# Second layer of a two-layer FFN as one scheme of 26 block products, its weight sums kept in device memory and streamed

## The chip, the cores and the metric

One core of a Trainium2 chip runs the whole program. The metric is device microseconds of one execution. The kernel before takes 1073.24 us, the median of 7 runs (1072.73 to 1074.44). Five engines run side by side: PE (TensorE, matmuls), DVE (VectorE), ACT (ScalarE), POOL (GpSimd) and SP (SyncE, which only issues DMAs here). Each executes its own instructions in the order of the program, and waits on semaphores for the others. DMAs are issued from a queue of SP, POOL or ACT, in order, and land later.

## The reference

```
kv  = einsum('bhsd,bhse->bhde', k, v)          # 8 batches, 8 heads, 576 tokens, 64 dims
o   = einsum('bhsd,bhde->bhse', q, kv)
x   = o / sqrt(mean(o*o, -1) + 1e-6) * g_norm  # then (B,H,S,D) -> (4608, 512)
h   = sigmoid(x @ w_gate) * (x @ w_val)        # 512 -> 1536
out = h @ w_out                                # 1536 -> 512
```

Everything is float32 on the chip; the three weights arrive as 64-bit floats and are converted.

## The kernel before

The 4608 tokens are nine chunks `c` of G = 512. Attention makes x, transposed, chunk by chunk (`feed`); chunk 0 is computed plainly, with the weights converted beside it. From chunk 1 on both layers use sums of blocks, so that fewer products are needed, as in Strassen's scheme and its kin: one 2x2 scheme of seven products, with a further level on one of them.

The first layer (`first_layer_fast`, loop `f` = 0..5, a "pass" each) makes two blocks of h at a time, `f` and `f + 6`, each [128 features, 512 tokens], in 24 matmuls of 256 columns and 7 of 128. Its sums of w_gate and w_val are made once, on POOL, in chunk 1 (`w_sum`, `w_sums2`, lines 729 to 746), stored in device memory (`kept`, `kept2`) and loaded again for every pass of later chunks (`load_sums`, L724 to L727, DMAs of 1 MB and 256 KB on POOL's queue). One addition of each pass is on POOL (L836); it waits for ACT's copies (L835), and DVE's L844 waits for it, and PE for that. The blocks end with products by the sigmoid on DVE (`end`, L800) and additions out of PSUM (L796). Then `h_sum` and `h_sums` (L880 to L889) make the sums of h for the second layer, four DVE operations of 128x256 a pass.

The second layer (`second_layer_fast`) has 60 matmuls of 256 columns and 42 of 128 a chunk (L920, L979); the small ones need sums that POOL makes during this stage (`sums2`, L909, 48 operations of 128x128). The sums of w_out (`t2w`, L1099 to L1106) are made once, on DVE, during chunk 1's first layer, and stay on the core. The last chunk has its own form, `second_layer_last`, with 72 matmuls of 256 columns and 24 of 128, ordered so that little is left to store at the end.

Beside this, the attention of a later batch is fed in steps: `fill` is a list of small steps, and `slot()` emits the next of them at marked places of both layers. A step on PE is the kv group (L355, L361) or one of two groups of 144 small matmuls (L396). `load_late` loads k and v of batch c + 2 at the end of a second layer, on SP's queue behind the stores of the results (`store`, L500). Tiles `gv`, `s12`, `s4` and `kv` come from one rotating pool of 21 buffers (`hp`), the tiles of the results and of the gates from `sg_tile` (5 buffers). PSUM banks are handed around by `take` and `give`: a bank is reused when DVE or ACT has read it.

What sets the order is thus the program's order on each engine, with these steps spread in it by hand; there is no scheduler (`manual_schedule`).

## Time and profile before

| | us |
|---|---|
| median of 7 runs | 1073.24 |
| the profiled execution | 1074.33 |
| its span, first to last instruction | 1072.5 |
| PE busy | 1059.7 |
| DVE busy | 671.6 |
| POOL busy | 311.8 |
| ACT busy | 307.4 |
| moved by DMA | 127.94 MB, mean 119 GB/s |

Line numbers (L753) are those of the kernel before. Names stand as out<-in. A float32 matmul shows as two MATMUL records, and each record's end is modelled, so that the distance of starts, not the length of a record, is its price. "Idle before" is the time for which an engine had nothing to run, with what ended it. SPq and POOLq are the issuing queues. The granted clock of PE is 1.00 in all windows.

### The profile page before, as it was taken

The numbers are of one execution on the slowest core, as the hardware profiler recorded it, in microseconds if no ns is written. First come the engines' busy times: TensorE is split into PE (matmuls) and PEld (weight loads), VectorE is DVE, ScalarE is ACT, GpSimd is POOL, SyncE is SP. The second block draws the span as 40 slices with busy tenths as digits, with TensorE's granted clock in tenths as the row PEclk, the third lists the DMA queues.
The fourth block names the chain that finished last, engine by engine and source line by source line (L and its number), as shares of the span: only waits on it lengthen the run. The fifth ranks groups of instructions, "written<-read, shape, count | busy, mean of one in ns | idle before, by whom it ended". The sixth has DMA issues, their size and how long they took to land.

```text
span 1072.5 us, 20227 instructions
## 1 busy us (share of the span) xinstructions
PE 1059.7 (99%) x7766; PEld 890.5 (83%) x7766; DVE 671.6 (63%) x1545; ACT 307.4 (29%) x737; POOL 311.8 (29%) x576
## 2 busy tenths in 40 slices
PE   8999999999999999999999999999999999999998
PEld 7644448788988898889988898889888988898887
DVE  4787766996556646675568466755566466626641
ACT  3654322331133303331243123311333032102210
POOL 0000045888111531145112711181115211631100
PEclk9999999999999999999999999999999999999999
DMA  9944712234433426341634263334333232312201
GB/s 247 265 158 156 237 62 96 99 123 139 138 114 121 133 63 198 111 133 41 182 110 135 80 186 101 121 96 122 126 123 120 55 106 99 99 40 99 99 1 39
DMA packets 85056, 127.94 MB, mean 119 GB/s; under 512 B 26976, under 2 KB 66272, under 8 KB 82272
## 3 DMA queue, kind: packets, MB, share of 16 engines
q1 hardware_dynamic: 70112, 63.66, 21.3%
q0 software_dynamic: 14496, 62.92, 17.1%
q8 instruction: 61, 1.00, 0.4%
q14 instruction: 35, 0.29, 0.1%
q10 hardware_dynamic: 352, 0.07, 0.0%
HBM read 102.24 MB, written 17.30 MB: 111 GB/s over the span
## 4 chain that ended last, share of the span: by engine, by line
PE 95%; DVE 2%; POOL 1%; DMA 1%; SPq 1%; issue 0%; POOLq 0%; DVEq 0%
PE mm L753 45%; PE mm L920 17%; PE mm L558 7%; PE mm L757 7%; PE mm L979 6%; PE mm L655 4%; PE mm L1030 3%; PE at L396 2%; PE at L355 1%; DMA v<-in_v_dram 1%; PE at L558 1%; PE two L262 0%; POOL tws L744 0%; PE two L292 0%; PE two L319 0%
## 5 line engine op out<-in xcount | busy, mean ns | idle before, releaser
L753 PE MATMUL mm<-xT,w 128*128 128x256 f32 x720 | 177.2, 379 | 0.0
L753 PE MATMUL mm<-sx,w 128*128 128x256 f32 x720 | 177.1, 379 | 0.0
L753 PEld LDWEIGHTS mm<-xT,w 128*128 128x128 f32 x720 | 133.0, 190 | 16.5 <-issue 0.5
L753 PEld LDWEIGHTS mm<-sx,w 128*128 128x128 f32 x720 | 132.0, 190 | 15.3
L836 POOL TENSOR_TENSOR sg<-sg 128x256 f32<-128x256 f32 x48 | 34.8, 724 | 322.6 <-ACT sg L835 303.1
L753 PE MATMUL mm<-xT,tws 128*128 128x256 f32 x432 | 113.1, 384 | 1.1 <-DVE gv L776 0.6
L753 PE MATMUL mm<-sx,tws 128*128 128x256 f32 x432 | 111.3, 380 | 0.1
L766 ACT COPY sg<-mm 128x256 f32<-128x256 f32 x96 | 36.0, 375 | 241.9 <-PE mm L753 241.5
L772 DVE TENSOR_TENSOR gv<-mm,sg 128x256 f32<-128x256 f32 x96 | 40.3, 423 | 91.6 <-PE mm L753 85.2
L753 PEld LDWEIGHTS mm<-xT,tws 128*128 128x128 f32 x432 | 77.1, 190 | 13.0 <-issue 3.0
L791 ACT ACTIVATE sg<-sg 128x256 f32<-128x256 f32 x96 | 40.0, 416 | 158.1 <-DVE sg L790 157.8
L753 PEld LDWEIGHTS mm<-sx,tws 128*128 128x128 f32 x432 | 75.7, 191 | 8.0 <-PE mm L753 1.2
L800 DVE TENSOR_TENSOR gv<-gv,sg 128x256 f32<-128x256 f32 x192 | 80.2, 438 | 0.0
L558 PE MATMUL mm<-xT,w 128*128 128x512 f32 x176 | 77.4, 594 | 0.0
L920 PE MATMUL mm<-w,s 128*128 128x256 f32 x336 | 73.7, 379 | 0.0
L920 PEld LDWEIGHTS mm<-w,s 128*128 128x128 f32 x336 | 63.8, 190 | 8.7
L776 DVE TENSOR_TENSOR gv<-mm,sg 128x256 f32<-128x256 f32 x96 | 40.5, 422 | 45.0 <-PE mm L753 39.1
L558 PEld LDWEIGHTS mm<-xT,w 128*128 128x128 f32 x176 | 32.6, 190 | 37.4 <-issue 35.9
L744 POOL TENSOR_TENSOR tws<-w 128x256 f32<-128x256 f32 x24 | 19.4, 827 | 151.9 <-DVE w L202 146.9
L790 DVE TENSOR_TENSOR sg<-mm,sg 128x256 f32<-128x256 f32 x96 | 40.3, 420 | 33.2 <-PE mm L753 32.8
L776 DVE TENSOR_TENSOR gv<-mm,gv 128x256 f32<-128x256 f32 x96 | 40.6, 423 | 27.7 <-PE mm L753 26.4
L757 PEld LDWEIGHTS mm<-xT,w 128*128 128x128 f32 x276 | 43.0, 191 | 6.6 <-DVE gv L796 3.3
(158 smaller groups left out, 1835.5 us busy)
## 6 DMA issues: line engine op xcount, KB each, us to landing
w<-kept POOLq DMA_DIRECT2D x21, 1024.0 KB, 6.1
tws<-kept POOLq DMA_DIRECT2D x21, 1024.0 KB, 5.2
out_dram<-sg SPq DMA_DIRECT2D x110, 64.0 KB, 1.7
q<-in_q_dram SPq DMA_DIRECT2D x24, 288.0 KB, 3.1
st<-in_moe_w_gate_dram SPq DMA_DIRECT2D x12, 512.0 KB, 3.7
st<-in_moe_w_val_dram SPq DMA_DIRECT2D x12, 512.0 KB, 7.7
st<-in_moe_w_out_dram SPq DMA_DIRECT2D x12, 512.0 KB, 4.4
kv<-in_k_dram SPq DMA_DIRECT2D x24, 256.0 KB, 5.0
```

Of the source, the lines that this page charges most:

```text
L558: nc.tensor.matmul(self.ps[i], w[("wg", "wv")[i], self.f][:, m, :], xT[self.c][:, m, :], start=(m == 0), stop=(m == NMT - 1), skip_group_c ...
L655: nc.tensor.matmul(ps[t], gv[0, f][:, P * t:P * t + P], w["wo", f], start=(f == 0), stop=(f == NFT - 1), skip_group_check=True)
L753: nc.tensor.matmul(ps, wt[:, m, :], xs[:, m, :], start=(new and m == 0), stop=(m == NK - 1), skip_group_check=True)
L757: nc.tensor.matmul(ps, wt, xs, start=new, stop=True, skip_group_check=True)
L766: nc.scalar.copy(out=d["sg"][:, h2], in_=d["pa"])
L772: tt(out=d["h"][:, h1], in0=d["pb"], in1=d["sg"][:, h2], op=ALU.add)
L776: tt(out=d["h"][:, h2], in0=ps, in1=d.pop("u")[:, h2], op=ALU.add)
L790: tt(out=d["sg"][:, h2], in0=d["pb"], in1=d["sg"][:, h2], op=ALU.add)
L791: nc.scalar.activation(out=d["sg"][:, h2], in_=d["sg"][:, h2], func=AF.Sigmoid)
L800: tt(out=d["h"][:, h], in0=d["h"][:, h], in1=d["sg"][:, h], op=ALU.mult)
L920: nc.tensor.matmul(ps, hs[f], ws[:, f, :], start=(new and f == 0), stop=(f == NF2 - 1), skip_group_check=True)
L979: nc.tensor.matmul(ps, hs[j], ws[j], start=(new and j == 0), stop=(j == N3 - 1), skip_group_check=True)
```

## The change

From chunk 2 on the second layer is one scheme with h as 4x4 blocks (four token tiles of 128 by four groups of three feature blocks, numbers 4t + l) and w_out as 4x2 blocks: 26 products (`PRODUCTS`), each three matmuls of 256 columns. Each product reads a block or a sum of blocks of h (`H_SUMS`, 28 sums for each of three feature blocks `j`, 128x128, all on POOL) and a block or a sum of blocks of w_out (`W_SUMS`, 18 sums). The h sums are emitted two at a time at the places of the first layer (`step`), for j = 0 and 1, and three at a time between the first ten products for j = 2. The w_out sums are made on DVE during chunk 1's second layer and stored in device memory (`kept3`); each chunk streams them back in the order of the products, 384 KB each, into a ring of seven places (`ring`, `load_w`), on POOL's queue. Chunk 1's second layer becomes plain, 48 matmuls of 512 columns; `second_layer_last`, `sums2`, `h_sum`, `h_sums` of before, `t2w` and their steps are gone. The h blocks get fixed places (`h_main`, `h_more`), k and v use `h_more` too (`kv_place`), and `sg_tile` has 6 buffers.

```diff
-                mains[n, name] = t = hp.tile([P, G], FP32, tag="gv", name="kv")
+                mains[n, name] = t = kv_place(len(mains))
...
-        rest = hp.tile([P, G], FP32, tag="gv", name="kv")
+        rest = kv_place(len(mains))
...
+    N3 = NF2 // 2
+    def block(l, j):
+        return 2 * j + l % 2 + NF2 * (l // 2)
     def gv_tile(c, f):
-        gv[c, f] = hp.tile([P, G], FP32, tag="gv", name="gv")
+        e, r = divmod(f, NF2)
+        l, j = 2 * e + r % 2, r // 2
+        gv[c, f] = h_main[j][:, NT * l:NT * l + NT].rearrange("p t c -> p (t c)")
         return gv[c, f]
+    def kv_place(i):
+        return h_more.rearrange("p j s c -> p (j s c)")[:, G * i:G * i + G]
     def sg_tile():
-        return sb.tile([P, G], FP32, tag="sg", name="sg", bufs=5)
+        return sb.tile([P, G], FP32, tag="sg", name="sg", bufs=6)
...
-                hp = ctx.enter_context(tc.tile_pool(name="hp", bufs=21))
+                hp = ctx.enter_context(tc.tile_pool(name="hp", bufs=1))
+                h_main = [hp.tile([P, 4 * NT, P], FP32, name=f"h{j}") for j in range(N3)]
+                h_more = hp.tile([P, N3, 3 * NT, P], FP32, name="h_more")
...
+        def step():
+            slot()
+            for _ in range(2):
+                if h_fill:
+                    h_fill.popleft()()
...
             if load:
                 load_sums(c + (n == 0), n)
-            slot()
+            if c == 2 and f:
+                for n_ in range(f, NR + 1, NF2 - 1):
+                    load_w(n_ - 1)
+            step()
...
             p6(two)
-            slot()
+            step()
...
-            h_sum(c, f)
             p3(two)
-            slot()
+            step()
             end(one, h1)
             end(two, h1)
-            h_sums(c, f)
+            if c > 1 and f % 2:
+                h_fill.extend(h_sums(f // 2))
         if c + 1 < NG:
             load_sums(c + 1, 1)
...
+    H_SUMS = ((18, 5, 1, 6), (21, 0, -1, 2), (24, 8, 1, 21), (17, 9, -1, 13), (26, 14, -1, 17), (25, 1, 1, 18),
+              (16, 11, -1, 15), (23, 12, -1, 16), (30, 26, -1, 10), (33, 21, 1, 23), (19, 3, 1, 11), (27, 1, 1, 19),
+              (42, 12, 1, 15), (34, 13, 1, 27), (35, 14, 1, 34), (36, 1, 1, 3), (20, 4, -1, 6), (22, 12, 1, 20),
+              (29, 8, 1, 25), (41, 0, 1, 29), (37, 4, 1, 12), (28, 7, 1, 18), (40, 28, -1, 16), (38, 7, 1, 20),
+              (39, 19, 1, 38), (32, 1, 1, 5), (31, 17, -1, 22), (43, 10, -1, 24))
+    W_SUMS = ((9, 1, 0, 1, 4), (12, 1, 3, -1, 9), (22, 1, 7, 1, 12), (14, -1, 2, -1, 9), (23, 1, 6, -1, 14),
+              (8, 1, 5, -1, 6), (21, 1, 4, -1, 8), (16, 1, 1, 1, 8), (18, 1, 2, -1, 16), (15, 1, 3, -1, 0),
+              (20, 1, 8, -1, 15), (10, 1, 5, -1, 7), (13, -1, 1, -1, 10), (25, 1, 3, 1, 13), (11, 1, 0, 1, 2),
+              (17, 1, 1, -1, 11), (19, -1, 10, -1, 11), (24, 1, 1, 1, 5))
+    PRODUCTS = (("A", 8, 4, "o5=A"), ("C", 9, 1, "o4=C"), ("B", 18, 10, "o3=B"), ("A", 24, 14, "o1=A"),
+                ("C", 26, 16, "t8=C"), ("B", 25, 19, "o1=o1+B"), ("E", 23, 12, "t9=E"), ("C", 30, 6, "o5=o5-C"),
+                ("A", 33, 9, "t9=t9+A"), ("F", 27, 13, "t0=F"), ("E", 16, 22, ""), ("B", 19, 25, "t0=B-t0"),
+                ("H", 42, 3, "t9=t9-H o4=o4-t9 o0=t9+t0"), ("F", 35, 24, ""), ("G", 36, 7, "t1=G t1=F-t1"),
+                ("D", 20, 15, "o2=D"), ("G", 2, 23, "o1=G-o1 o2=o2+t0 o5=o5+t1 o7=t1-E"), ("D", 22, 20, "o3=o3+D"),
+                ("I", 41, 11, "o0=o0+I o1=o1-I"), ("E", 37, 21, ""), ("E", 40, 7, "o3=o3+E"), ("J", 39, 3, ""),
+                ("J", 32, 17, "o2=J-o2"), ("D", 31, 8, "t8=t8+D o7=o7-t8"), ("K", 43, 2, "o4=o4+K"),
+                ("H", 14, 18, "o6=H+t8"))
+    DONE = {18: 0, 22: 1, 24: 2, 25: 3}
+    LAST = {"A": 8, "B": 11, "C": 7, "D": 23, "E": 20, "F": 14, "G": 16, "H": 25, "I": 18, "J": 22, "K": 24}
+    def h_slots():
+        used, last = {p[1] for p in PRODUCTS}, {}
+        for n, (_, x, _, y) in enumerate(H_SUMS):
+            last[x] = last[y] = n
+        at = {4 * t + l: NT * l + t for t in range(NT) for l in range(4)}
+        spare = deque(at[v] for v in range(16) if v not in last and v not in used)
+        top = 16
+        for n, (v, x, _, y) in enumerate(H_SUMS):
+            spare.extendleft(at[u] for u in (y, x) if last[u] == n and u not in used)
+            if spare:
+                at[v] = spare.popleft()
+            else:
+                at[v], top = top, top + 1
+        assert top <= 16 + 3 * NT
+        return at
+    h_at = h_slots()
+    h_fill = deque()
+    def h_form(v, j):
+        s_ = h_at[v]
+        return h_main[j][:, s_] if s_ < 4 * NT else h_more[:, j, s_ - 4 * NT]
+    def h_sums(j):
+        return [lambda v=v, x=x, sign=sign, y=y: nc.gpsimd.tensor_tensor(
+            out=h_form(v, j), in0=h_form(x, j), in1=h_form(y, j), op=ALU.add if sign > 0 else ALU.subtract)
+            for v, x, sign, y in H_SUMS]
+    tok = [slice(P * i, P * i + P) for i in range(NT)]
+    def w_raw(v):
+        n, l = divmod(v, 4)
+        b0 = block(l, 0)
+        return w2[:, b0:b0 + NF2 - 1:2, DH * n:DH * n + DH]
+    STREAM = [p[2] for p in PRODUCTS if p[2] > 7]
+    NS = len(STREAM)
+    NR = 7
+    N_FAST = NG - 2
+    def ring(i):
+        i %= NR
+        return w_raw((0, 5)[i]) if i < 2 else w_ring[:, i - 2]
+    def load_w(i):
+        if i < N_FAST * NS:
+            nc.gpsimd.dma_start(out=ring(i), in_=kept3[i % NS].rearrange("p (j n) -> p j n", j=N3))
+    def w_forms():
+        last = {}
+        for n, (_, _, x, _, y) in enumerate(W_SUMS):
+            last[x] = last[y] = n
+        more = h_more.rearrange("p j s c -> p (j s c)").rearrange("p (i j n) -> p i j n", j=N3, n=DH)
+        spare = deque([w_ring[:, i] for i in range(NR - 2)] + [more[:, i] for i in range(2 * N3)])
+        at = {v: w_raw(v) for v in range(8)}
+        steps = []
+        for n, (v, sx_, x, sy, y) in enumerate(W_SUMS):
+            at[v] = spare.popleft()
+            for u in {x, y, v}:
+                if u > 7 and last.get(u, n) <= n:
+                    spare.append(at[u])
+            def make(v=v, sx_=sx_, x=x, sy=sy, y=y, o=at[v], a=at[x], b=at[y]):
+                op = ALU.add if sy > 0 else ALU.subtract
+                if sx_ > 0:
+                    tt(out=o, in0=a, in1=b, op=op)
+                else:
+                    nc.vector.scalar_tensor_tensor(out=o, in0=a, scalar=-1.0, in1=b, op0=ALU.mult, op1=op)
+                nc.gpsimd.dma_start(out=kept3[STREAM.index(v)].rearrange("p (j n) -> p j n", j=N3), in_=o)
+            steps += [make, idle]
+        return steps
+    def second_layer_plain(c):
+        for t in range(NT):
+            i = free.popleft()
+            ps = bank(i)
+            order_ = [block(l, j) for j in range(N3) for l in (0, 2, 1, 3)]
+            for f in order_:
+                nc.tensor.matmul(ps, gv[c, f][:, tok[t]], w2[:, f, :], start=(f == order_[0]), stop=(f == order_[-1]),
+                                 skip_group_check=True)
+                slot()
+            ot = sg_tile()
+            nc.scalar.copy(out=ot, in_=ps)
+            give(i)
+            store(c, t, ot)
+        flush()
+        load_late(c + 2)
     def second_layer_fast(c):
+        o = {}
+        tiles = [sg_tile() for _ in range(6)]
+        rows = [tiles[i] for i in (0, 1, 2, 4)]
+        for t in range(NT):
+            for n in range(2):
+                o[f"o{2 * t + n}"] = rows[t][:, DH * n:DH * n + DH]
+        for i, names in ((3, ("t8", "t9")), (5, ("t0", "t1"))):
+            for n, name in enumerate(names):
+                o[name] = tiles[i][:, DH * n:DH * n + DH]
+        regions, streamed = {}, count((c - 2) * NS)
+        state = {}
+        def product(i, js):
+            name, hv, wv, _ = PRODUCTS[i]
+            if i not in state:
+                if name not in regions:
+                    regions[name] = take() + (True,)
+                state[i] = next(streamed) if wv > 7 else None
+                new = regions[name][2]
+                regions[name] = regions[name][:2] + (False,)
+                state[i] = state[i], new
+            g, new = state[i]
+            ws = w_raw(wv) if g is None else ring(g)
+            for j in js:
+                nc.tensor.matmul(regions[name][1], h_form(hv, j), ws[:, j], start=(new and j == 0), stop=(j == N3 - 1),
                                  skip_group_check=True)
+        def finish(i):
+            name, _, wv, steps = PRODUCTS[i]
+            o.update({r: v[1] for r, v in regions.items()})
+            for step in steps.split():
+                out_, expr = step.split("=")
+                if expr in regions:
+                    nc.scalar.copy(out=o[out_], in_=o[expr])
+                else:
+                    sign = "+" if "+" in expr else "-"
+                    x, y = expr.split(sign)
+                    tt(out=o[out_], in0=o[x], in1=o[y], op=ALU.add if sign == "+" else ALU.subtract)
+            for r in list(regions):
+                if i == LAST[r]:
+                    give(regions.pop(r)[0])
+            g = state[i][0]
+            if g is not None:
+                load_w(g + NR)
+            if i in DONE:
+                t = DONE[i]
+                if c == NG - 1 and t == NT - 1:
+                    store(c, t, rows[t], slice(0, DH), (nc.sync, nc.scalar))
+                else:
+                    store(c, t, rows[t])
+            elif c == NG - 1 and i == 23:
+                store(c, NT - 1, rows[NT - 1], slice(DH, DM))
+        first = 3
+        for i in range(first):
+            product(i, range(N3 - 1))
+        for i in range(len(PRODUCTS)):
+            for _ in range(3):
+                if h_fill:
+                    h_fill.popleft()()
+            product(i, [N3 - 1] if i < first else range(N3))
+            finish(i)
...
+    kept3 = kept_pool.tile([NS, P, N3 * DH], FP32, name="kept3")
...
-    def t2w_sum(i, in0, in1):
-        for fs in (slice(f, f + 2) for f in range(0, NF2, 2)):
-            w2_sums.append(lambda fs=fs: tt(out=t2w[i][:, fs], in0=in0[:, fs], in1=in1[:, fs], op=ALU.subtract))
-
-    t2w_sum(3, b22, b12)
-    t2w_sum(1, b12, b11)
-    t2w_sum(2, b22, t2w[1])
-    t2w_sum(4, b21, t2w[2])
-
-
+    w_ring = sums.tile([P, NR - 2, N3, DH], FP32, name="w_ring", bufs=1)
...
         if c + 1 < B:
-            steps = feed(c + 1)
-            if c == 1:
-
-                i = 4
-                while w2_sums:
-                    steps.insert(i, (DVE, w2_sums.popleft()))
-                    i += 2
-            spread(steps, (1, 2, 3, 4, 5) if c == 1 else (2, 3, 4, 5))
+            spread(feed(c + 1), (1, 2, 3, 4, 5) if c == 1 else (2, 3, 4, 5))
         first_layer_fast(c)
         sums_of(c + 1)
-        (second_layer_fast if c < NG - 1 else second_layer_last)(c)
+        if c == 1:
+            fill.extend(w_forms())
+        (second_layer_plain if c == 1 else second_layer_fast)(c)
         flush()
```

## The prediction

> **What bounds the kernel.** I read the page's engine row and chain first, then the windows of the stages, then the chain in order of time for the price of one matmul record, and last the timelines of GpSimd (POOL) and SyncE.
>
> ```profile
> PE 1059.7 (99%) x7766; PEld 890.5 (83%) x7766; DVE 671.6 (63%) x1545; ACT 307.4 (29%) x737; POOL 311.8 (29%) x576
> ...
> PE 95%; DVE 2%; POOL 1%; DMA 1%; SPq 1%; issue 0%; POOLq 0%; DVEq 0%
> ```
>
> TensorE carries 95% of the chain, so the change is worth what it takes from PE's columns, less any new wait of PE. The windows are chunk 1's first and second layer, then the second layers of chunks 2, 7 and 8 (columns: length, then each engine's busy time):
>
> ```profile
> 161.59:245.14 83.55, 79.89 (x597) 67.10 (x596) 71.17 (x139) 27.54 (x77) 62.60 (x96) 1.00 0.32 114
> 245.14:283.35 38.21, 37.80 (x349) 33.94 (x348) 21.79 (x55) 4.14 (x8) 21.20 (x48) 1.00 0.31 91
> ...
> 360.27:397.77 37.50, 37.50 (x349) 33.99 (x348) 19.98 (x49) 4.06 (x7) 21.46 (x48) 1.00 0.32 87
> 924.83:960.27 35.44, 35.44 (x205) 32.34 (x204) 15.93 (x37) 1.35 (x4) 22.86 (x48) 1.00 0.15 47
> 1031.81:1068.41 36.60, 36.60 (x193) 32.69 (x191) 6.80 (x19) 1.49 (x4) 0.00 (x0) 1.00 0.10 24
> ```
>
> Second layers have no idle PE, and the granted clock is 1.00. The one stage with slack to win is chunk 1's first layer: 83.55 us, where chunk 2's takes 76.92 with the same matmuls plus one attention group (L396).
>
> ```profile
> 120.55 41.20 PE mm L655 x96
> ...
> 474.01 6.47 PE mm L920 x30
> 480.48 1.84 PE at L396 x130
> 482.32 19.62 PE mm L920 x90
> 501.94 9.63 PE mm L979 x84
> ```
>
> A float32 matmul is two records. One record costs 19.62 / 90 = 0.218 us (6.47 / 30 = 0.216) at 256 columns, 9.63 / 84 = 0.115 at 128, 41.20 / 96 = 0.429 at 512.
>
> **PE's columns.** Chunks 2 to 7: before, 120 records of 256 and 84 of 128, 25.9 + 9.6 = 35.5 (the window of chunk 7 says 35.44). After: 26 products of 3 matmuls, 156 records x 0.2157 = 33.65. That is -1.80 a chunk, **-10.8** for six (between -1.6 by the 0.218 and -1.9). Chunk 8: 36.60 becomes 33.65, **-2.95**. Chunk 1 becomes plain: 48 matmuls of 512 columns, 96 x 0.429 = 41.2, where the window of 38.21 less its attention group (37.50 - 35.44 = 2.06, by chunks 2 and 7) was 36.15: **+5.05**. The attention group is not lost: in the built order of PE both groups of chunk 1 now lie in its first layer, at the same cost.
>
> **Chunk 1's first layer.** Its PE work is six passes of 11.96 us (24 matmuls of 256, 7 of 128), 2.4 for kv and 1.73 for one group: 75.9. So 7.7 us are waits. The chain names them, first VectorE (DVE), at the end POOL:
>
> ```profile
> 188.58 1.40 DVE w L1101
> ...
> 240.21 0.72 POOL w L727
> 240.94 0.74 POOL sg L836
> ...
> 241.71 0.29 DVE sg L844
> ```
>
> The change takes from DVE there the four h sums (L880 to L889: 0.56 + 0.41 + 2.04 + 0.41) and two w_out sums (L1101, 1.3 to 1.6) of each pass, about 6 of 13.7 us, so the DVE wait (three passes of some 1.7) goes. What is late next is POOL: its sums of w_gate and w_val stay. Without contention a pass of it is 4 x 2.29 (pair 1.41, wait 0.30, DMA issue 0.56) + 2.82 + 0.70 = 12.7 against 13.7 now and PE's 12. From its free start at 171.95, L836 of the last pass would end at 237.0 instead of 241.7. The DVE's four two-input products a pass still collide; in proportion (4 of 10 collisions) 1.9 of the 4.7 stays: 238.9. PE's last pass would start at 227.3 with both attention groups ahead of it and needs L836 about 8.65 later, at 235.95. The wait left is 3.0: **-4.7** (between 0, POOL as slow as now, and -7.7).
>
> **The h sums on POOL.** 28 sums x 3 blocks of 128x128 a chunk; two thirds go beside the first layer, the last 28 beside the products.
>
> ```profile
> 474.59 1.90 POOL L909 TENSOR_TENSOR gv<-t2w 128x128 f32<-128x128 f32 x3 [0.89 <-PE mm L920]
> ...
> 486.92 5.16 POOL L909 TENSOR_TENSOR gv<-gv 128x128 f32<-128x128 f32 x12
> ...
> 460.66 0.92 POOL L726 DMA_DIRECT2D w<-kept  x1 [4.65 <-PE mm L753]
> 461.57 0.71 POOL L727 DMA_DIRECT2D w<-kept  x1
> ```
>
> A free sum costs 5.16 / 12 = 0.43, one against DVE's two-input operations 1.90 / 3 = 0.63. Nine of 28 follow their own operand at once, where such a pair (L734 at 159.01 and 159.56) shows 0.55; so 0.47 on average. First layer, one pass: 14 x 0.47 + 4 x 0.2 of collisions + L836 0.72 + loads 1.63 = 9.7 of 12 us. Queued behind them is L836, which waits for ACT until 5.1 to 5.5 us into the pass; loads end 0.65 into it and four sums at 2.7, so it is not late, and L844 and PE do not feel it. Even at 0.63 it is 11.2. Cost nothing; cover gone, each us over 12 costs PE 1 us a pass. DVE gains some 1.7 us a pass and loses 4 x 0.26 (products of 0.41 took 0.67 in that stretch): nothing on PE in chunks 2 to 8, where it waited for no DVE.
>
> The trace's collision is 0.26 for DVE and 0.2 for POOL. [...]
>
> **The streamed sums.** 18 loads of 384 KB a chunk, ring of seven; the load into a slot is queued on POOL behind the product that used it, and the remaining sums behind that load's wait. The tightest is product 17: its load (slot freed by product 8) stands behind 27 sums and 5 loads. POOL can start when DVE's last products are done, 1.85 us into the stage (475.5, without L880, against 473.84). 1.85 + 27 x 0.47 + 5 x 0.65 (0.56 to 0.92) = 17.8. Landing is placed between two rows:
>
> ```profile
> tws<-kept POOLq DMA_DIRECT2D x21, 1024.0 KB, 5.2
> ...
> kept<-tws POOLq DMA_DIRECT2D x24, 256.0 KB, 2.7
> ```
>
> so 3.1 for 384 KB: 20.9. PE arrives at 17 x 1.294 = 22.0, in chunks 2 to 6 at 24.0 behind the attention group. Slack 1.1 and 3.1. Every sum itself is ready 1 us or more ahead. Chunk 7 also has DVE's x sums early (about 1 us of collisions). I take **+0.8** for PE's waits here (between 0 and the first rival's price). PSUM handovers: ACT copies (0.375) follow PE by 0.03 and have 0.86 us at the closest place; nothing, at worst 0.2 a chunk.
>
> **Edits hidden.** The 18 w_out sums with their stores move into chunk 1's second layer: DVE 18 x about 0.95 (between 0.68 for 512 columns, L695, and 1.22 for 1024, L189) = 17, POOL 18 x 0.56 = 10, under 41 us of PE; uncovered they would delay chunk 2's first products. Seven first loads in chunk 2: 0.6 to 0.9 each on POOL, at most two a pass. kv goes to fixed places, which the last products free, so its loads wait for the end of the stage on SP's queue. They did so before: behind the stores, issue from 515.66, landed by 527.1, needed by PE (L355) at 529.95.
>
> ```profile
> 519.76 1.36 SPq L119 DMA_DIRECT2D kv<-in_k_dram  x2
> ...
> 1066.22 3.60 SPq L500 DMA_DIRECT2D out_dram<-sg  x8
> ```
>
> Two of four tiles' stores now leave earlier, so kv starts about 1 us earlier. Nothing; cover gone, 1 us for each us beyond 2.8, five times.
>
> **The tail.** A store issue takes 3.60 / 8 = 0.45 on SP. Before, PE's last record ends at 1068.41, SP's last issue starts 1.0 later and lands at 1070.9. After, SP issues 14 stores from 3.45 us ahead of PE's end (after products 22, 23, 24, 25), so the last starts 2.4 after it: **+1.5** (0.8 to 2.5).
>
> **Sum.** -10.8 - 2.95 + 5.05 - 4.7 + 0.8 + 1.5 = **-11.1**. The profiled execution took 1074.33 (span 1072.5 and 1.8 around it): 1063.2. It stands 1.1 above the median of 1073.24, so the median would be 1062.1; I say 1062.
>
> **Rivals.**
> - *POOL too slow for the stream; slower.* If the sums beside the products cost 0.63, as at 474.59, and a load 0.92, as at 460.66, product 17's load is issued at 1.85 + 27 x 0.63 + 5 x 0.92 = 23.5 and landed at 26.6: late by 4.6 in chunks 7 and 8 and 2.6 in five others, 22 us: 1083. It cancels the gain where waits reach 12 us, POOL 3.1 us late without an attention group, 0.63 a sum alone. For it: all sums run on one in-order queue between loads that wait. Against: 0.63 is shown only where DVE runs two-input operations without a pause, and DVE has few in this stage.
> - *The stream lands late.* 7.1 MB in 33.6 us is 211 GB/s, where these windows moved 47 to 91. If a load lands after 6 us rather than 3.1 (a megabyte took 5.2), chunks 7 and 8 lose 1.8 each, the rest little, and with queueing up to 1 us in each: 1066 to 1070. For it: seven loads in a burst when POOL catches up. Against: the first slice of the run moved 247 to 265 GB/s.
> - *Chunk 1's first layer keeps its waits*, POOL being as slow as now: 1066.8.
> - *The h sums' move by itself does nothing* for chunks 2 to 8, since DVE hides them already; that is in the sum.
>
> [...] Here 0.43 stands against DVE's 0.28 for 128x128. [...]
>
> **How the numbers follow.** Forecast, with the third rival as its upper end, 0.66 (1057 to 1067); late landing 0.18; POOL too slow 0.16. About 0.2%, 2.1 us, is what can be told from no change. The low end: no wait left in chunk 1's first layer (-3), no stall (-0.8), tail 0.8 (-0.7): 1057.5, and 1 for rounding of the rates. The high end takes in late landing, leaving most of the first rival out: 1071.5. Faster: forecast, late landing nearly whole: 0.81. Within 0.2%: 0.05, slower 0.14, both from the first rival and mixtures.
>
> **What would show it.** Second layers of chunks 2 to 6 of 35.7 us and of 7 and 8 of 33.7, with PE never idle for a streamed load (DMA) or for POOL; chunk 1's second layer 41.2, its first 80.6 with both attention groups; L836 waiting for ACT in every pass from chunk 2 on; last issue of SP 2.4 us after PE. Wrong if PE waits at products 17 to 19 for w_ring, or if DVE waits at L844's place for POOL.

## The result and the profile after

The changed kernel takes 1067.41 us, the median of 14 runs (1065.51 to 1071.54), beside 1073.17 for the kernel before on the same chips (34 runs, 1071.48 to 1075.1): a ratio of 0.9953, 95% interval 0.9945 to 0.9961. It is 5.8 us faster, where 11.1 were forecast (1062 us). The profiled execution took 1066.52, its span is 1064.7. From here on line numbers are those of the changed kernel: L766 and L770 are the first layer's matmuls, L1034 the second layer's, L999 chunk 1's plain ones, L944 the sums of h, L966 the streamed loads, L1047 the additions that empty the products' PSUM, L706 to L719 the sums of x.

The engine row and the two chain rows of the changed kernel's page:

```profile
PE 1050.2 (99%) x7334; PEld 856.8 (80%) x7334; DVE 601.0 (56%) x1340; ACT 322.4 (30%) x772; POOL 505.5 (47%) x972
...
PE 87%; DMA 6%; POOL 2%; DVE 2%; SPq 1%; issue 1%; ACT 0%; POOLq 0%; DVEq 0%
PE mm L766 42%; PE mm L1034 18%; PE mm L571 7%; PE mm L770 6%; PE mm L670 4%; PE mm L999 4%; DMA xT<-xTs 4%; PE at L399 2%; DMA h_more<-in_v_dram 2%; POOL tws L757 1%; PE at L358 1%; DVE sg L1047 1%; PE at L571 1%; PE two L295 1%; DMA h_mor
```

PE still carries the chain, but 87% of it and not 95%: DMA holds 6%, most of it the transfer `xT<-xTs`, which brings a later chunk's x and which the change does not touch. The windows (length, busy time of PE, PEld, DVE, ACT, POOL; granted clock, DMA share, GB/s) of chunk 1's two layers, the second layers of chunks 2 and 3, both layers of chunk 4, and the second layers of chunks 7 and 8:

```profile
159.42:241.60 82.18, 80.15 (x741) 69.46 (x740) 48.60 (x118) 31.37 (x81) 60.09 (x96) 1.00 0.38 127
241.60:282.80 41.20, 41.20 (x97) 18.24 (x96) 23.60 (x37) 1.83 (x4) 9.77 (x18) 1.00 0.67 240
359.12:394.82 35.70, 35.70 (x302) 31.32 (x300) 15.65 (x37) 6.08 (x12) 22.81 (x45) 1.00 0.88 263
...
472.23:507.88 35.65, 35.65 (x301) 31.27 (x300) 15.12 (x36) 6.08 (x12) 22.24 (x45) 1.00 0.86 256
507.88:586.47 78.59, 76.80 (x597) 68.23 (x596) 47.13 (x123) 28.74 (x77) 37.98 (x75) 1.00 0.46 149
586.47:623.75 37.28, 35.77 (x301) 31.23 (x300) 18.03 (x43) 6.08 (x12) 22.51 (x45) 1.00 0.85 255
919.70:954.32 34.62, 34.12 (x158) 29.48 (x157) 14.64 (x32) 3.35 (x9) 24.44 (x45) 1.00 0.68 230
1025.86:1059.69 33.83, 33.83 (x157) 29.45 (x155) 9.19 (x24) 3.35 (x9) 18.53 (x39) 1.00 0.46 146
```

Where it runs undisturbed, the second layer is what the columns said: 35.70, 35.65 and 33.83 us, and 41.20 for chunk 1. Its DMA share went from 0.32 (chunk 2, before) to 0.88. The gaps lie elsewhere, and the waits of PE behind chunk 1 name them (total us, times, longest):

```profile
PE mm L770 <- DVE sg L1047: 2.0, 3, 0.9
PE mm L1034 <- issue: 1.5, 1, 1.5
PE at L364 <- DMA h_more<-in_v_dram: 1.2, 2, 0.9
PE mm L1034 <- DVE sg L1047: 0.5, 1, 0.5
```

L770 are small matmuls near the start of the next chunk's first layer; they wait for a PSUM bank that DVE has not emptied yet (L1047, the second layer's additions). All stages together, from the two traces' first PE records (us; "forecast" is the row before plus the prediction's terms):

| | before | forecast | after |
|---|---|---|---|
| chunk 1, first layer (after: with one attention group more, about 2) | 83.55 | 80.6 | 82.18 |
| chunk 1, second layer | 38.21 | 41.2 | 41.20 |
| first layers of chunks 2 to 8 | 525.3 | 525.3 | 528.3 |
| second layers of chunks 2 to 8 | 259.8 | 246.8 | 248.6 |
| PE's last record to the end | 4.12 | 5.6 | 5.06 |

The sum of these changes is -5.6 measured and -11.4 forecast (0.3 more than the prediction's -11.1, which took the moved attention group at 2.06 in one place and at 1.73 in the other). The span is 2.2 us shorter beyond that only because the profiled execution's first stage began at 22.2 instead of 24.4, ahead of anything that changed.

Why DVE is late, in chunk 3's second layer (timeline of DVE: start, length, then in brackets the idle time before and what ended it):

```profile
499.02 0.75 DVE L1047 TENSOR_TENSOR sg<-sg,mm 128x256 f32<-128x256 f32 x2 [0.84 <-PE mm L1034]
505.50 0.69 DVE L706 TENSOR_TENSOR sx<-xT 128x512 f32<-128x512 f32 x1 [5.74 <-DMA xT<-xTs]
506.23 0.69 DVE L707 TENSOR_TENSOR sx<-sx,xT 128x512 f32<-128x512 f32 x1
506.84 0.41 DVE L1047 TENSOR_TENSOR sg<-sg,mm 128x256 f32<-128x256 f32 x1
```

DVE stands 5.74 us at the first sum of the next chunk's x, because `xT` has not landed; the additions of the last products are queued behind it in order, and the stores behind those. Such waits at L706 make 19.6 us in five chunks. In the kernel before, the same transfers in the corresponding 18 us (489.6 to 507.6) landed after 2.0 to 2.1 us; now (488 to 506) they take 7 to 8. DMA rows of that stretch (number, size of each, median us from issue to landing), before, then after:

```profile
DMA packets 961, 0.61 MB, mean 34 GB/s; under 512 B 448, under 2 KB 960, under 8 KB 960
...
xT<-xTs SPq DMA_DIRECT2D x4, 72.0 KB, 2.1
xT<-xTs SPq DMA_DIRECT2D x4, 64.0 KB, 2.0
```

```profile
DMA packets 1779, 4.60 MB, mean 255 GB/s; under 512 B 586, under 2 KB 1029, under 8 KB 1778
...
w_ring<-kept POOLq DMA_DIRECT2D x10, 384.0 KB, 6.5
...
xT<-xTs SPq DMA_DIRECT2D x4, 72.0 KB, 8.1
xT<-xTs SPq DMA_DIRECT2D x4, 64.0 KB, 7.0
```

### The profile page after: what moved, and what is told of

It reads as the page before. It is cut to its first block, busy times and chain, and to the rows that moved or that the text cites. A ratio compares the mean times of both kernels' runs of the same rounds, so it can differ in the third digit from the quotient of the medians.

```text
span 1064.7 us, 19454 instructions
## 1 busy us (share of the span) xinstructions
PE 1050.2 (99%) x7334; PEld 856.8 (80%) x7334; DVE 601.0 (56%) x1340; ACT 322.4 (30%) x772; POOL 505.5 (47%) x972
## 4 chain that ended last, share of the span: by engine, by line
PE 87%; DMA 6%; POOL 2%; DVE 2%; SPq 1%; issue 1%; ACT 0%; POOLq 0%; DVEq 0%
PE mm L766 42%; PE mm L1034 18%; PE mm L571 7%; PE mm L770 6%; PE mm L670 4%; PE mm L999 4%; DMA xT<-xTs 4%; PE at L399 2%; DMA h_more<-in_v_dram 2%; POOL tws L757 1%; PE at L358 1%; DVE sg L1047 1%; PE at L571 1%; PE two L295 1%; DMA h_more<-in_k_dram 0%
## 5 line engine op out<-in xcount | busy, mean ns | idle before, releaser
L766 PE MATMUL mm<-xT,w 128*128 128x256 f32 x720 | 177.4, 379 | 0.0
L766 PE MATMUL mm<-sx,w 128*128 128x256 f32 x720 | 177.1, 379 | 0.0
L766 PEld LDWEIGHTS mm<-xT,w 128*128 128x128 f32 x720 | 133.4, 190 | 17.6 <-issue 1.0
L766 PEld LDWEIGHTS mm<-sx,w 128*128 128x128 f32 x720 | 132.0, 190 | 15.3
L785 DVE TENSOR_TENSOR h<-mm,sg 128x256 f32<-128x256 f32 x96 | 40.8, 425 | 147.9 <-PE mm L766 147.9
L766 PE MATMUL mm<-xT,tws 128*128 128x256 f32 x432 | 112.5, 383 | 0.0
L766 PE MATMUL mm<-sx,tws 128*128 128x256 f32 x432 | 111.1, 380 | 1.1 <-issue 1.1
L1034 PE MATMUL mm<-w,h 128*128 128x256 f32 x390 | 91.0, 379 | 0.0
L944 POOL TENSOR_TENSOR h<-h 128x128 f32<-128x128 f32 x189 | 88.4, 481 | 2.8
L813 DVE TENSOR_TENSOR h<-h,sg 128x256 f32<-128x256 f32 x192 | 86.1, 469 | 0.0
L766 PEld LDWEIGHTS mm<-xT,tws 128*128 128x128 f32 x432 | 77.8, 190 | 9.5
L766 PEld LDWEIGHTS mm<-sx,tws 128*128 128x128 f32 x432 | 75.9, 191 | 8.2 <-issue 1.3
L1034 PEld LDWEIGHTS mm<-w,h 128*128 128x128 f32 x390 | 74.1, 190 | 10.1
L1047 DVE TENSOR_TENSOR sg<-sg,mm 128x256 f32<-128x256 f32 x77 | 31.1, 418 | 78.5 <-PE mm L1034 78.1
L944 POOL TENSOR_TENSOR h_more<-h 128x128 f32<-128x128 f32 x126 | 60.0, 482 | 28.8 <-DVE h L813 25.5
L966 POOL DMA_DIRECT2D w_ring<-kept x90 | 49.8, 554 | 48.6 <-PE mm L1034 48.3
L1034 PE MATMUL mm<-w_ring,h_more 128*128 128x256 f32 x300 | 70.8, 380 | 1.5 <-issue 1.5
```

What stands on the lines that cost most here:

```text
L766: nc.tensor.matmul(ps, wt[:, m, :], xs[:, m, :], start=(new and m == 0), stop=(m == NK - 1), skip_group_check=True)
L785: tt(out=d["h"][:, h1], in0=d["pb"], in1=d["sg"][:, h2], op=ALU.add)
L813: tt(out=d["h"][:, h], in0=d["h"][:, h], in1=d["sg"][:, h], op=ALU.mult)
L944: return [lambda v=v, x=x, sign=sign, y=y: nc.gpsimd.tensor_tensor(out=h_form(v, j), in0=h_form(x, j), in1=h_form(y, j), op=ALU.add if sig ...
L966: nc.gpsimd.dma_start(out=ring(i), in_=kept3[i % NS].rearrange("p (j n) -> p j n", j=N3))
L1034: nc.tensor.matmul(regions[name][1], h_form(hv, j), ws[:, j], start=(new and j == 0), stop=(j == N3 - 1), skip_group_check=True)
```

## The experiments

Theory T: PE's gain is all there, and the streamed loads take half of it away again by slowing other transfers. Rivals: R1, POOL's work itself (its sums, its collisions with DVE); R2, PE waiting for the streamed loads; R3, chunk 1's first layer. All runs were timed against the kernel before. The first four ran together.

**The changed kernel again.**

> The changed kernel once more, as it is, for a second profile beside the experiments. Theory T (the columns that PE saves are all there, and some 5 us are lost again because the streamed loads fill the DMA engines in the second layers, to a share of 0.85 to 0.88, so that the transfers xT<-xTs land after 5.5 us instead of 2.1 and DVE, standing in order behind them at the sums of x, holds up the additions that empty PSUM): 1066 to 1069, the sums of x (L706) waiting for xT by several us in most second layers from chunk 2 to 6, second layers of 35.7. The gap of 1.51 us that PE has in chunk 4's second layer ahead of product 6, for which the profile names no cause: absent if it is chance (then chunk 4's second layer is 35.7 and this run is about 1.5 faster), there again if it belongs to the program.

1066.54 us (1065.68 to 1070.84), ratio 0.9947 (0.9933 to 0.9961). The waits at L706 are there again, in other sizes (23.3 us in five), and PE's waits behind chunk 1 make 5.6 us. The gap in chunk 4 is there too, 1.13 us at the same product, so it is no single accident. It does not come every time: four of the profiles further down, with the same groups of matmuls, have none over 0.25 us there.

**A third of the streamed bytes.**

```diff
-            nc.gpsimd.dma_start(out=ring(i), in_=kept3[i % NS].rearrange("p (j n) -> p j n", j=N3))
+            js = slice(0, N3 if i < NR else 1)
+            nc.gpsimd.dma_start(out=ring(i)[:, js], in_=kept3[i % NS].rearrange("p (j n) -> p j n", j=N3)[:, js])
```

> Every streamed load but the first seven brings one of its three blocks (128 of 384 KB); two thirds of the bytes are left out, and the products read old values there. The number of loads, their places in POOL's order, what they wait for and all sums stay. T: the DMA share of the second layers falls to about 0.45, xT<-xTs lands after 2 to 3 us, the waits of DVE at L706 and of PE at the starts of chunks 3 to 7 go, and the time is 1061 to 1063. Rival R1 (POOL: its sums beside the products, their collisions with DVE, and its loads' issues are what costs): nothing of it is changed, so 1066 to 1068. Rival R2 (PE waits for the streamed loads themselves): also 1061 to 1063, but then the profile of the changed kernel should show PE waiting for w_ring, which it does for less than 1 us. Rival R3 (the loss is chunk 1's first layer): 1066 to 1068.

1060.65 us (1059.33 to 1061.49), ratio 0.9881 (0.9869 to 0.9894). The DMA share of chunk 3's second layer is 0.51, L706 waits once, 1.2 us, and behind chunk 1 PE waits for nothing that another engine or a transfer releases. All POOL sums and issues are still there, and chunk 1's first layer takes as long as in the changed kernel (82.37), so R1 and R3 fall as the cause of the loss behind chunk 1: it comes from the transfers. R2 is not told apart by this run; the traces of the unpaced kernels name `w_ring` as what PE waited for in chunk 7 alone (0.4 to 1.4 us in three of them).

**The sums of x behind the last addition.**

```diff
-        sums_of(c + 1)
+        late_sums = 1 < c and c + 1 < B
+        if not late_sums:
+            sums_of(c + 1)
...
         flush()
+        if late_sums:
+            x_ = x_sums(c + 1)
+            for n in (0, 1, 4, 5, 2, 3, 6, 7):
+                x_[n]()
```

> The sums of x for chunks 3 to 7 (L706 to L719) are put on DVE behind the last addition of the second layer, where the changed kernel has them between the additions of products 20 to 25; of the eight, the four whose results are used first come first. Nothing is left out. T: DVE doesn't stand still ahead of an addition that empties PSUM any more, rows are stored some 4 us earlier, and the waits of PE at the starts of chunks 3 to 7 go, but for what the sums of x now come late themselves: 1063 to 1066. If the late xT transfers cost as much in their new place: 1066 to 1068. R1 and R3: 1067, and with the sums in a worse place up to 1070.

1063.67 us (1061.45 to 1064.30), ratio 0.9907 (0.9894 to 0.9920). The `xT` transfers are as late as ever (7.6 and 6.8 us in the stretch above), but nothing is queued behind them, and first layers of 76.06 to 76.33 follow. That DVE stands in order ahead of the additions is thus worth 2.9 us of the loss by the medians on the same chip (1066.54 to 1063.67), 4.3 by the ratios. One wait behind chunk 1 is left that is longer than 0.4 us. It is in chunk 7, ahead of product 18, and its releaser is a streamed load:

```profile
PE mm L1034 <- DMA w_ring<-kept: 1.3, 1, 1.3
```

**Without the last 28 sums of h.**

```diff
-            if c > 1 and f % 2:
+            if c > 1 and f % 2 and f // 2 < N3 - 1:
                 h_fill.extend(h_sums(f // 2))
```

> The last 28 sums of h of each chunk from 2 on, those that POOL makes beside the products, are left out (84 sums become 56); the products read old values in their place. All streamed loads stay with all their bytes, and POOL issues each as soon as a product has freed its place, evenly over the stage instead of in bursts. T, with the bytes as the cause: the mean DMA share of the second layers stays at 0.85, xT<-xTs still lands after 4 us or more, DVE still waits at L706, and the time falls by 0 to 2, 1065 to 1067; if the bursts rather than the mean are the cause, xT lands after 3 us and it is 1062 to 1064. R1: the whole loss comes back, 1061 to 1063, with xT as late as before. R3: 1067.

1063.88 us (1062.38 to 1065.43), ratio 0.9915 (0.9902 to 0.9927). The DMA share of chunk 3's second layer is 0.88, as high as before, and yet the waits at L706 fall to 8.4 us. So it is not the mean load of the DMA engines alone. The `xT` transfers are still late: 5.2 and 4.1 us as medians of the whole run (72 and 64 KB), for 5.4 and 5.9 in the changed kernel. What differs is when POOL issues the loads, and the next run keeps the sums and changes that alone.

**The sums paced.** In the changed kernel POOL is behind with its sums until 18 us into the stage, and then issues at once what had been free for long (timeline of POOL, chunk 3):

```profile
489.25 0.59 POOL L966 DMA_DIRECT2D w_ring<-kept  x1
489.86 0.47 POOL L944 TENSOR_TENSOR h<-h,h_more 128x128 f32<-128x128 f32 x1
490.25 1.64 POOL L966 DMA_DIRECT2D w_ring<-kept  x3
492.80 0.54 POOL L966 DMA_DIRECT2D w_ring<-kept  x1 [0.91 <-PE mm L1034]
```

Five loads, 1.9 MB, in 4 us, at 489 to 493; SP issues the `xT` transfers from 491.2 on. The edit:

```diff
-            for _ in range(3):
-                if h_fill:
-                    h_fill.popleft()()
+            while h_fill and len(H_SUMS) - len(h_fill) < 6 + i + i // 6:
+                h_fill.popleft()()
```

> The same 28 sums of h beside the products, all made, but paced on POOL: six ahead of product 0 and then about one and a sixth a product, instead of three a product until they run out at product 9. So each streamed load stands behind few sums and is issued about when a product has freed its place, as in the run without these sums (1063.9), and not in bursts of five when POOL has caught up. T, now with the bursts as a part of the cause: xT<-xTs in chunks 2 to 6 no longer than in the run without the sums (5.2), the sums of x wait less for it (8.4 us in all there, 19.6 in the changed kernel), 1063 to 1065. R1 (it is POOL's work itself, its collisions with DVE, and not when the loads go): nothing is taken from POOL, so 1066 to 1068. A sum that is now too late for its product would show as PE waiting for h_more, and 1067 to 1072.

1060.82 us (1059.97 to 1062.76), ratio 0.9885 (0.9872 to 0.9897): as good as with two thirds of the bytes left out, but with every byte and every sum still there. The same places in its trace, POOL, then the window of the stage, then DVE:

```profile
489.08 0.56 POOL L966 DMA_DIRECT2D w_ring<-kept  x1 [0.23 <-PE mm L1034]
489.66 0.47 POOL L944 TENSOR_TENSOR h_more<-h 128x128 f32<-128x128 f32 x1
490.37 0.56 POOL L966 DMA_DIRECT2D w_ring<-kept  x1 [0.25 <-PE mm L1034]
...
492.96 0.56 POOL L966 DMA_DIRECT2D w_ring<-kept  x1 [0.36 <-PE mm L1034]
```

```profile
472.40:508.04 35.64, 35.64 (x301) 31.26 (x300) 18.80 (x43) 6.09 (x12) 23.13 (x45) 1.00 0.90 269
```

```profile
500.25 0.98 DVE L706 TENSOR_TENSOR sx<-xT 128x512 f32<-128x512 f32 x1 [0.32 <-DMA xT<-xTs]
```

These loads wait for PE (the brackets), that is, each goes when its place is freed. The DMA share is even higher, 0.90, but `xT` lands after 6.0 and 3.7 us instead of 8.1 and 7.0, and L706 waits 0.32 us instead of 5.74 (8.2 instead of 19.6 in all chunks). Bytes and sums are unchanged, so the bursts are what cost the time. T stands with that correction. The run without the sums stays 3 us behind this one by the median, though it has less to do and its waits at L706 are the same (8.4 and 8.2). The two profiled executions can't explain it: they took 1062.40 and 1062.76 us, and the former shows one wait of 1.65 us for a kv load. So what the pacing is worth beyond spreading the loads stays open.

**Chunk 1: the sum of g2 on DVE.**

```diff
-            nc.gpsimd.tensor_tensor(out=g2[:, h1], in0=g2[:, h1], in1=g2[:, h2], op=ALU.add)
+            (nc.vector if c == 1 else nc.gpsimd).tensor_tensor(out=g2[:, h1], in0=g2[:, h1], in1=g2[:, h2], op=ALU.add)
```

> In chunk 1 alone the sum of the two halves of g2 (L858) is made on DVE instead of POOL. The prediction's step was that POOL, with the sums of w_gate and w_val, is what PE waits for in chunk 1's first layer, by way of this sum. If so, the stage of 82.2 us falls to 78 to 79.5 (77.6 is its PE work with both attention groups), and the time by 2.5 to 4: 1063 to 1065. If PE's waits there came from something else than POOL, 1066 to 1068, and the stage stays at 81 to 82. If POOL is late for the next pass's own weights all the same, 0.73 a pass is what it gains: five passes, 1063 at best, with PE waiting for tws.

1068.37 us (1065.80 to 1071.65), ratio 0.9954 (0.9939 to 0.9969), the stage 82.08: nothing gained. DVE, then POOL, in one pass (timelines):

```profile
208.19 1.99 DVE L858 TENSOR_TENSOR sg<-sg 128x256 f32<-128x256 f32 x1
210.11 0.41 DVE L859 TENSOR_TENSOR sg<-mm,sg 128x256 f32<-128x256 f32 x1
```

```profile
208.48 1.42 POOL L757 TENSOR_TENSOR tws<-w,tws 128x256 f32<-128x256 f32 x2
```

The sum with both operands in SBUF takes 1.99 us and is not done before POOL's pair of subtractions is (it ends at 210.18, the pair at 209.90); the operation after it, of the same size but with one operand in PSUM, takes 0.41. In the kernel before, L880, a sum of this size with both operands in SBUF too, takes 0.42 to 0.57. So POOL, which had been late for this sum, now seems to hold DVE at it: POOL's second subtraction follows the first, two in 1.42 us, and DVE's sum ends behind both. The trace does not show why.

**Chunk 1: a sum of the weights on DVE.** The base of this run and of the next is the combined kernel, described further below, with chunk 1's sum of g2 back on POOL.

```diff
-            nc.gpsimd.tensor_tensor(out=t[:, i - 1, e], in0=b[in0],
-                                    in1=b[in1] if isinstance(in1, tuple) else t[:, in1 - 1, e], op=ALU.subtract)
+            (nc.vector if f and i == 3 else nc.gpsimd).tensor_tensor(
+                out=t[:, i - 1, e], in0=b[in0], in1=b[in1] if isinstance(in1, tuple) else t[:, in1 - 1, e],
+                op=ALU.subtract)
```

> The combined kernel (sums of x last, paced sums of h), but chunk 1's sum of g2 back on POOL, and in its place the third of the four sums of w_gate and w_val that chunk 1 makes for each next pass (two 128x256 subtractions of L757 of five passes, raw operands) on DVE; their store stays on POOL's queue. It takes 1.4 to 1.7 of some 13 us a pass from POOL and puts 0.8 on DVE. If POOL's length of pass is what chunk 1's first layer waits for: the stage falls from 82.2 to 79 to 80, the time to 1057 to 1059. If the cause is that DVE's operation with two SBUF inputs stands still while POOL's pairs run (1.99 us for the sum of g2 in place of 0.41), DVE's new subtractions pay that as well, hold up the additions behind them that empty PSUM, and the stage stays at 82 or grows to 84: 1060 to 1063.

1060.36 us (1059.55 to 1063.02), ratio 0.9887 (0.9871 to 0.9902), the stage 81.16, between the two expectations. The time is no better than that of the same kernel without this edit (ratio 0.9874 in the run on the tail below, which differs otherwise by the tail's edit alone). DVE's longest operations with two SBUF operands in the stage take 2.05 and 2.18 us, and PE waits for DVE there (1.1 us in two waits).

**Chunk 1: two sums of the weights left out.**

```diff
-        for e in range(2):
+        for e in range(0 if f and i > 2 else 2):
```

> The combined kernel with chunk 1's sum of g2 back on POOL; of the four sums of w_gate and w_val that chunk 1 makes for each of the next five passes, the subtractions of the third and the fourth are left out (their stores stay and write what lies in the tile). POOL's pass falls by 2.9 us and nothing is put on another engine. If POOL in chunk 1's first layer is what the prediction missed by: the stage falls from 82.2 to its PE work of 77.6 (to 78.2 with a rest), the time to 1055.5 to 1057. If PE waits there for something else: it stays at 81 to 82, 1059 to 1061.

1057.25 us (1056.57 to 1060.35), ratio 0.9863 (0.9845 to 0.9880), the stage 78.51, and all that PE's waits list there is 0.2 us:

```profile
PE mm L766 <- issue: 0.2, 1, 0.2
```

The changed kernel's 82.18 holds a gap of 1.12 without a releaser (see the attention groups below), and this run's 78.51 one of 0.24. Less these the stage falls from 81.06 to 78.27. So 2.8 us of it hang on POOL's sums, which the prediction had as the bound of this stage. The time alone can't show it: the ratio's interval overlaps that of the run on the tail (0.9859 to 0.9889). Of the two attempts to put the work elsewhere, neither shows a gain in the time.

**The sums of h on DVE.** The base is again the changed kernel.

```diff
-        return [lambda v=v, x=x, sign=sign, y=y: nc.gpsimd.tensor_tensor(
+        return [lambda v=v, x=x, sign=sign, y=y: nc.vector.tensor_tensor(
```

> All 84 sums of h of each chunk from 2 on are made on DVE instead of POOL, at the same places of the program. Worked out: 84 x 0.28 = 23.5 us of DVE a chunk, in the first layer 14 x 0.28 = 3.9 more in a pass of 12 us where DVE has about 7.2 of work, in the second layer 28 x 0.28 = 7.8. POOL then only issues loads there, each when its product has freed the place, as in the run without the last sums. T: with the loads spread, 2 to 3 of the lost time come back, less what DVE's sums hold up of its own additions, each 0.28 and at most 3 ahead of one that empties PSUM: 1063 to 1066. [...] If DVE, in order behind its sums and behind the late xT, is what PE waits for: 1068 to 1080.

1069.79 us (1066.80 to 1071.57), ratio 0.9962 (0.9947 to 0.9976). The first layers of chunks 4 to 6 go to 76.96, where 76.06 is undisturbed, and PE waits for DVE's own evacuations:

```profile
PE mm L766 <- DVE h L789: 1.7, 5, 0.3
```

The loads are spread here as well and L706 waits only 7.8 us, and still it is no better than the changed kernel (0.9962 beside 0.9953, the intervals overlap) and 9 us slower than the paced one. A single sum is shorter on DVE (0.28 against 0.48 us), and yet the time gains nothing by the move. DVE's order holds operations that PE waits for; the trace names 1.7 us of such waits, and the first layers of chunks 2 to 8 are 4.7 us longer in all than in the paced run (529.2 beside 524.5). Gaps without a releaser make 3.2 us behind chunk 1, beside 1.8 in the paced run. The rest of the 9 us is not accounted for.

**Combined.** The edits are the late sums of x (for chunk 8 too), the paced sums of h, and the g2 sum on DVE, on the changed kernel:

> Three edits together, nothing left out: the sums of x behind the second layer's last addition (now for chunk 8 as well), the paced sums of h, and chunk 1's sum of g2 on DVE. T with the two terms that were missed: 1067.0 less 3.4 for the sums of x, less 0 to 1 for the pacing beside it, less 2.5 to 4 in chunk 1: 1058.5 to 1061.5. If the gains of the first two are the same microseconds and chunk 1 gives nothing: 1063 to 1064. No better than the changed kernel, 1066 or more: then the late transfers only move their price.

1059.91 us (1058.47 to 1061.01), ratio 0.9874 (0.9859 to 0.9888). From chunk 2 on PE has no gap over 0.25 us; second layers take 35.59 to 35.69 and 33.67 to 33.83. Chunk 1 stays at 82.39. The gains of the two edits overlap: beside the pacing, the late sums of x are worth some 0.9, within the spread of the runs.

**The tail.**

```diff
-                    store(c, t, rows[t])
+                    store(c, t, rows[t], queues=(nc.sync, nc.scalar) if c == NG - 1 and t else (nc.sync,))
...
-                store(c, NT - 1, rows[NT - 1], slice(DH, DM))
+                store(c, NT - 1, rows[NT - 1], slice(DH, DM), (nc.sync, nc.scalar))
```

> The combined kernel with chunk 1's sum of g2 back on POOL; the last chunk's stores of the rows that come last are dealt to SP's and ACT's queues in turn instead of SP's alone. The tail from PE's last record to the end (5.06 in the changed kernel, 4.12 before; the prediction said 1.5 longer) falls by 0.5 to 1.0 if the queue of stores on SP is what makes it longer, and stays at 5.1 if it is the last product's own chain of copy, addition, store and landing. The time 1059.3 to 1060.3 in either case, so the answer is in the profile's last microseconds.

The tail falls from 5.1 to 3.69 us, by more than expected and to less than before the change (4.12): it was SP's queue of stores. The time, 1059.34 (1058.17 to 1061.02), ratio 0.9874 (0.9859 to 0.9889), can't be told from the combined kernel's; both beat the kernel before and the changed one.

**The attention groups in halves.** The trace's DMA records hold instruction queues too. One of them (q8) brought 58 packets of 16 KB in the changed kernel, whose PE has 14,668 matmul and weight-load records: 253 for each packet (61 and 15,532 before: 255). By these counts, which give an estimate only, an attention group of 144 matmuls and as many weight loads, 288, is more than one packet's worth. The profiles of the kernel before, the changed one and the runs above hold 27 gaps of PE over 0.25 us within or less than 5 us behind the short matmuls of an attention group (L399, 144 of them in 1.8 us), all but a few without a releaser; in every one PE resumes 1.25 to 1.62 us after a 16 KB packet of that queue has ended. In the changed kernel's chunk 4 the packet ends at 596.31, and PE starts again at 597.86. The gap of chunk 1 in the run on the tail (timeline of PE), and the packet in the microsecond from 196.2 on (packets, MB, share of the 16 engines):

```profile
192.55 1.80 PE L399 MATMUL at<-kvq,qTs 32*64 32x64 f32 x144
...
195.47 1.03 PE L766 MATMUL mm<-xT,tws 128*128 128x256 f32 x4
198.65 1.86 PE L766 MATMUL mm<-sx,tws 128*128 128x256 f32 x4 [2.15 <-issue]
200.31 1.87 PE L766 MATMUL mm<-xT,tws 128*128 128x256 f32 x4
```

```profile
q8 instruction: 1, 0.02, 6.0%
```

This gap, the longest, costs more than its 2.15 us. Four records take 1.86 us behind it instead of 1.03: the granted clock is 0.50 from 198.6 to 202.0 (0.98 over the stage), which is 1.7 us more; the stage takes 84.50 in this profile. Behind the changed kernel's gaps of 1.12 and 1.51 us, and behind one of 1.78 in the paced run, the clock is 1.00. The edit, without the idle steps that go:

```diff
-            def u_mm():
-                d["u"] = u = at_ps()[:, 0:NQ, 0:2 * QC]
-                for which in range(2):
+            def u_mm(which):
+                if which == 0:
+                    d["u"] = at_ps()[:, 0:NQ, 0:2 * QC]
+                u = d["u"]
...
-            return ([(PE, u_mm), (ACT, u_square), (DVE, lambda: u_sum(0)), (DVE, lambda: u_sum(1)), (ACT, u_root),
+            return ([(PE, lambda: u_mm(0)), (PE, lambda: u_mm(1)), (ACT, u_square), (DVE, lambda: u_sum(0)), (DVE, lambda: u_sum(1)), (ACT, u_root),
...
```

> The combined kernel with the tail on two queues, and each attention group of 144 small matmuls on PE (L399, 1.8 us) cut into two halves of 72 that go into neighbouring slots, with other matmuls between them; an idle slot after each is dropped. Nothing is left out. In every profile from the changed kernel on, PE stands still for 1.1 to 2.2 us behind the second such group of chunk 1's first layer, and in most for 0.8 to 1.8 us behind the group in chunk 4's second layer, with no releaser; each of these gaps ends 1.25 to 1.6 us after a 16 KB packet of the instruction queue has ended. If the cause is that a group's short instructions use PE's stock of instructions up faster than a packet brings new ones: the gap at 196 us falls below 0.5, chunk 1's first layer from 81.2 to 84.5 in the runs so far to 79.5 to 81, and the time from 1059.3 to 1057 to 1058.5. If the gap has another cause: it stays at 1.1 to 2.2, and the time at 1059 to 1060.5.

This profile has no such gap, there or elsewhere (timeline of PE; the lines are two or three further down in this kernel):

```profile
194.37 1.05 PE L401 MATMUL at<-kvq,qTs 32*64 32x64 f32 x72
195.36 1.13 PE L769 MATMUL mm<-xT,tws 128*128 128x256 f32 x4
196.32 1.03 PE L769 MATMUL mm<-sx,tws 128*128 128x256 f32 x4
197.19 1.03 PE L769 MATMUL mm<-xT,tws 128*128 128x256 f32 x4
```

But the time is 1063.44 us (1061.53 to 1064.42), ratio 0.9916 (0.9902 to 0.9929). Chunk 1's first layer takes 81.80, not the 79.5 to 81 expected. A group in two halves costs 0.43 us more (second layers 36.03 for 35.60, first layers 76.50 for 76.07), about 5 for the twelve groups, where the gaps are worth some 2 to 4. The remedy is dearer than the harm. That PE runs out of instructions there is the author's reading. The packets ahead of all 27 gaps support it; that the gaps are missing in this one profile says less, since the run with two sums left out has uncut groups and no gap over 0.25 us either.

## Why the prediction was half right

The forecast was 1062 us, and half of the gain came. The step that failed is the price of the streamed loads. Two rows of the kernel before that bear on it (loads of 256 KB, issued behind loads of 1 MB on the same queue; number, size, median us to landing):

```profile
w<-kept POOLq DMA_DIRECT2D x21, 256.0 KB, 5.9
txs<-kept POOLq DMA_DIRECT2D x21, 256.0 KB, 5.3
```

- **PE's columns, -10.8 and -2.95: right.** 35.6 to 35.7 and 33.7 to 33.8 us wherever nothing disturbs, chunk 1's plain layer 41.20 where 41.2 was said.
- **Waits for the streamed loads, +0.8: the step that failed.** Two things in it were wrong. The landing was "placed between two rows" at 3.1 us; it is 5.1 as a median and 6.5 in the burst. One of the two rows, `kept<-tws`, is of stores into device memory, and the price of a load was taken without the others in flight. The loads of 256 KB above, 5.3 and 5.9, were nearer to what came. And the step asked only who waits for the loads. PE does so a little, as the prediction's own sign of being wrong said (products 17 to 19), but only in chunk 7, ahead of product 18: 0.5 us in this profile, 1.3 in the run with the late sums of x, where the releaser is named. That stage takes 34.62 here and 33.67 in the paced run. With 6.5 in place of 3.1 the prediction's own sum has the tightest load landing at 24.3 us, behind the 22.0 of that chunk. Those who pay are the other transfers: `xT`, 2.0 to 2.1 before, 7.0 to 8.1 in the same place, and through DVE's order the additions, the stores and the kv loads. That is 2.0 us of PE at the chunk starts, 1.2 at kv, and 0.5 in chunk 7. This price, too, stood in the trace of the kernel before: beside its 1 MB loads (462 to 478 us) `xT` of 64 KB landed after 5.0 us instead of 2.0.
- **"kv loads: nothing"** failed by the same. The slack of 2.8 us was computed from landings of the kernel before, and it went twice, by 0.3 and 0.9.
- **The late-landing rival (1066 to 1070)** named the time and, in the burst "when POOL catches up", the cause. Its mechanism was another, PE waiting at the tightest product, which chunk 7 alone shows. That its time fits is partly luck: 2.6 us of the loss are stalls that no rival had. The argument against it was a rate of 247 to 265 GB/s, and rate is not what ran out: the paced run's window moves 269 GB/s with PE never idle.
- **Chunk 1's first layer, 80.6: 82.18.** POOL is the bound there, as said. The part that was not in the sum is the stall behind the second attention group, put down to instructions, which the change moves into this stage: 1.12 in this profile, 0.24 to 2.2 over the others. Less this stall the stage takes 80.9 to 81.1 us in the seven profiles that have all these sums on POOL, uncut groups and the full clock, so the forecast of 80.6 is met within 0.5. The same stall in chunk 4 adds 1.5.
- **The h sums on POOL, nothing: right**, at 0.48 us a sum for the 0.47 taken. POOL being too slow for the stream (the slower rival) did not come: its last sum ends 18.1 us into the stage of chunk 3, where 17.8 were worked out for the load behind it, and the loads behind the sums are late for PE only in chunk 7.
- **The tail, +1.5: +0.94.** SP's last stores were the right place; SP's last issue starts 2.6 us after PE's last record (2.4 were said, 1.0 before), but only 0.94 of that shows at the end.

Terms missed: 3.7 for the transfers, of which the sum had 0.8; 1.5 and 1.1 for the stalls behind attention groups; 0.5 of POOL in chunk 1; the tail gives 0.6 back. That is 5.4 of the 5.8 between the two sums.

## What to carry to other kernels

When a change adds a stream, its price is not only whether its consumer is in time: list every other transfer in flight in that stretch, and take its landing from rows of the same direction that ran beside such a load, not from quiet stretches (here 5.3 and 5.9 us in such rows, where 3.1 was assumed and 5.1 came). Keep a stream's issues from bunching, by pacing what stands ahead of them on their queue (1066.5 to 1067.4 us became 1060.8), and do not put an operation that waits for a transfer ahead of the ones that free PSUM (2.9 us by the medians). If a gap has no releaser behind a run of many short instructions, look at the instruction queue (a 16 KB packet ended 1.25 to 1.62 us before PE went on), and at the granted clock behind the gap (0.50 in one case).

## What the hardware showed that was not expected

- The same bytes at a like DMA share (chunk 3's second layer) cost some 6 us or almost nothing, by when they are issued: 0.86 in bursts (1066.5 to 1067.4 us), 0.90 paced (1060.8), beside 1060.7 with two thirds of them left out.
- PE stands still behind 144 short matmuls: 27 gaps of 0.3 to 2.2 us, each ending 1.25 to 1.62 us after a 16 KB instruction packet. The kernel before has such gaps too (0.56 at its L396). Behind the longest of them, 2.15 us, the granted clock was 0.50 for 3.4 us.
- With both operands in SBUF a DVE operation of 128x256 took 1.99 us beside a back-to-back pair on POOL, where one of the same size with an operand in PSUM took 0.41 right behind it; in the run with a sum of the weights on DVE the longest two with both operands in SBUF took 2.05 and 2.18.
